# Turning the second matmul of a fused attention and feed-forward kernel round: W1 stationary, 512 tokens moving, and the output turned back by VectorE, copies and GpSimd

## Chip, cores, metric

One core of one Trainium2 chip. The metric is the device time of one execution in microseconds (us), lower is better. A run is called slow when it is over 1.5% above the fastest of the same kernel; such runs do occur on some chips at a lower granted clock, and verdicts use the fast runs alone. A verdict of "faster" or "slower" needs 2%.

## The reference, cut to what matters

```python
x: (4, 12480, 128)   inducing: (32, 128)   w_in: (128, 2048)   w_out: (2048, 128)   alpha: (2048,)

def mab(q, kv):                       # one attention head, softmax over kv
    a = softmax(q @ kv.T / sqrt(128));  return a @ kv
h   = mab(inducing, x)                # 32 rows per batch
y   = mab(x, h).reshape(49920, 128)
hid = y @ w_in
out = (maximum(hid, 0) + alpha * minimum(hid, 0)) @ w_out
```

The kernel uses that y = (softmax weights over 32) @ h. It forms hW = h @ w_in once per batch, so that a hidden unit is a sum over 32 scores only, and splits the activation into alpha * hid (a linear term, folded into one 32 x 128 matrix hA) and (1 - alpha) * max(hid, 0), whose scale is folded into W1. The softmax denominator is applied to the output at the end.

## The kernel before

Tokens are worked in groups of 512, four groups to a block of 2048, six blocks and a remainder of 192 tokens to a batch, four batches. A group takes four fills. A fill makes four PSUM banks of hidden units (each a 32-row matmul of 512 tokens; four run at once in the four row strips of the array), which ScalarE or VectorE evict with a ReLU into `gt`, and then multiplies the `gt` of the fill before with W1.

```python
def fill(st, g, j):                                # first matmul: hidden units x 512 tokens
    for r in range(4):
        ps = bank()
        mm(ps[:, :512], st.hW[32*r : 32*r+32, j, :], rep[32*r : 32*r+32, :512])
    # ... four evictions ps -> gt[:, r, :], split between ScalarE and VectorE by a plan

def mm2(st, g, j, gt):                             # second matmul: 16 of 128 columns
    for r in range(4):
        for k in range(NB):                        # NB = 4 blocks of 128 tokens
            mm(acc[:, k, :], gt[:, r, k*128 : k*128+128], W1[:, r*NJ + j, :], ...)

def finish(st, g):                                 # tokens are on partitions: scale and store
    nc.vector.tensor_tensor(out=ob, in0=acc, in1=rbc, op=MULT)        # 1 / denominator
    (nc.sync if last_one else nc.gpsimd).dma_start(out=dst, in_=ob)   # 256 KB a group

def a_load(st, u):                                 # x of the next batch, a block of 2048 tokens
    nc.gpsimd.dma_start(out=xn, in_=src)
def a_xpose(st, u):                                # the same, transposed: xT
    nc.sync.dma_start_transpose(out=st.xT[:, u], in_=xn)
def b_rep(st, s):                                  # scores, replicated to four row strips
    for r in range(4): nc.sync.dma_start(out=rep[32*r : 32*r+32], in_=e2d)

# when (in groups, k = 2 i of the batch before):  a_load at k, a_xpose at k + 3,
#   a_scores (TensorE reads xT) at k + 5, its transposed scores e1T through SyncE, a_accum at k + 8;
#   b_scores(s) and its store e2d at group 4 s - 4, b_rep at 4 s - 3, first use at group 4 s
```

Every engine's order is fixed by the program (`pin`), also that of the DMAs in the queues of SyncE and GpSimd.

The softmax here doesn't subtract the row's maximum and nothing guards it: scores larger than these inputs give would overflow.

Of the kernel before, what the change touches and what calls it, by code (L numbers as in the profile page):

```python
# [15 lines left out]
P = 128  # L16
NB = 4
GRP = P * NB
NQ = 4
# [5 lines left out]
def kernel(  # L25
# [30 lines left out]
    def pin(bi):  # L56
# [18 lines left out]
    gt_pool = ctx.enter_context(tc.tile_pool(name="gtp", bufs=4))  # L75
    head_pool = ctx.enter_context(tc.tile_pool(name="headp", bufs=3))
    rep_pool = ctx.enter_context(tc.tile_pool(name="repp", bufs=3))
    dram = ctx.enter_context(
        tc.tile_pool(name="e2d", bufs=3, space=bass.MemoryType.DRAM)
    )  # L80
    ob_pool = ctx.enter_context(tc.tile_pool(name="obp", bufs=3))
    psum = ctx.enter_context(
        tc.tile_pool(name="ps", bufs=1, space=bass.MemoryType.PSUM)
    )
# [16 lines left out]
    def new_batch(b):  # L101
        st = Batch()
        st.b = b
        st.xT = xt_pool.tile([C, NS, NQ, GRP], bf16, name="xT", tag="xT")
        st.xTr = xt_pool.tile([C, JR, PR], bf16, name="xTr", tag="xTr")
        st.xn = {}
        st.e1T = {}
        st.sc = scale
        st.rs = None
        st.e2 = {}  # L110
        st.d = {}
        st.rep = {}
        st.rden = {}
        if b > 0:
            st.es = work.tile([P, NS + 1], f32, name="es", tag="es")
            st.hacc = work.tile([P, C], f32, name="hacc", tag="hacc")
            nc.vector.memset(st.es[:], 0.0)
            nc.vector.memset(st.hacc[:], 0.0)
        return st
# [266 lines left out]
    def b_den(st, s):  # L386
        e2 = st.e2.pop(s)
        ps = bank()
        if s < NS:
            for j in range(NB):  # L390
                mm(ps[:, j * NQ : (j + 1) * NQ], e2[:, j * P : (j + 1) * P], pick[:])
            rd = work.tile([P, NB, NQ], f32, name="rd", tag="rd")
            pin(nc.vector.reciprocal(
                out=rd[:].rearrange("p j q -> p (j q)"), in_=ps[:, : NB * NQ]
            ))
        else:
            for j in range(JR):
                mm(ps[:PR, j : j + 1], e2[:, j * PR : (j + 1) * PR], pick[0:M, 0:1])
            rd = work.tile([PR, JR, 1], f32, name="rdr", tag="rdr")
            pin(nc.vector.reciprocal(  # L400
                out=rd[:].rearrange("p j q -> p (j q)"), in_=ps[:PR, :JR]
            ))
        st.rden[s] = rd
# [3 lines left out]
    def shape_of(g):  # L407
        return (P, NB, 1) if g < NS * NQ else (PR, JR, 2)

    held = []  # L410

    def flush():
        while held:
# [31 lines left out]

    def mm2(st, g, j, gt):
        pp, nb, cp = shape_of(g)
        acc = accs[(st.b * NG + g) % 2]
        begun = (g % 2 == 1 and st.b + g > 1) or cp > 1
        for r in range(4):  # L450
            for i in range(cp):
                c = r * NJ + j * cp + i
                for k in range(nb):
                    k0 = (i * nb + k) * pp
                    mm(
                        acc[:pp, k, :], gt[:, r, k0 : k0 + pp], W1[:, c, :],
                        start=(j == 0 and r == 0 and i == 0 and k == 0 and not begun),
                        stop=False, skip_group_check=True,
                    )
        if j == NJ // cp - 1 and st.b * NG + g > 0:  # L460
            held.append((st, g))
# [7 lines left out]
        return []  # L469

    def linear(st, groups):
        for k in range(NB):
            for r, g in enumerate(groups):
                pp, nb, cp = shape_of(g)
                if k < nb:
                    mm(
                        accs[(st.b * NG + g) % 2][:pp, k, :],
                        st.rep[g][32 * r : 32 * r + 32, k * pp : (k + 1) * pp],
                        st.hA[32 * r : 32 * r + 32, :],
                        start=((r == 1 or cp > 1) and k == 0), stop=False, skip_group_check=True,  # L480
                    )

    def finish(st, g):
        pp, nb, _ = shape_of(g)
        acc = accs[(st.b * NG + g) % 2]
        s, q = divmod(g, NQ)
        rd = st.rden[s]
        rq = rd[:, :, q : q + 1]
        rbc = bass.AP(tensor=rq.tensor, offset=rq.offset, ap=[rq.ap[0], rq.ap[1], [0, C]])
        ob = ob_pool.tile([P, NB, C], f32, name="ob", tag="ob")  # L490
        pin(nc.vector.tensor_tensor(  # L491
            out=ob[:pp, :nb, :], in0=acc[:pp, :nb, :], in1=rbc, op=MULT
        ))
        t0 = st.b * N + s * SUP
        if s < NS:
            dst = out[t0 : t0 + SUP, :].rearrange("(p q j) c -> q p j c", q=NQ, j=nb)[q]
        else:
            dst = out[t0 : t0 + REM, :].rearrange("(p j) c -> p j c", j=nb)
        last_one = (st.b, g) == (B - 1, NG - 1)
        pin((nc.sync if last_one else nc.gpsimd).dma_start(out=dst, in_=ob[:pp, :nb, :]))  # L500
        st.rep.pop(g)



    order = [0, 1, NS] + list(range(2, NS))
    st = new_batch(0)
    ind_f = const.tile([M, C], f32, name="ind_f")
    xs = const.tile([P, NQ, GRP], f32, name="xs")
    src = x[0, 0:SUP, :].rearrange("(p q j) c -> p q (j c)", q=NQ, j=NB)
    pin(nc.sync.dma_start(out=xs[:, 0:2, :], in_=src[:, 0:2, :]))  # L510
    pin(nc.scalar.dma_start(out=xs[:, 2:4, :], in_=src[:, 2:4, :]))
# [11 lines left out]
    for u in order[3:]:  # L523
        a_load(st, u, pieces=2)
    w_in_b = const.tile([C, DFF], bf16, name="w_in_b")
    w_out_f = const.tile([P, KC, C], f32, name="w_out_f")
    pin(nc.gpsimd.dma_start(out=w_in_b[:], in_=moe_w_in))
    w_out_v = moe_w_out.rearrange("(r j p) c -> p r j c", p=P, j=NJ)
    w_out_g = w_out_f[:].rearrange("p (r j) c -> p r j c", j=NJ)
# [150 lines left out]
    def make_plan():  # L680
# [3 lines left out]
        for i, (b, g, j) in enumerate(fills):  # L684
            pp, nb, cp = shape_of(g)
            w = pp * nb * cp
            ca, cd = w * 0.75 + 96, w * 1.04 + 68
            lin = 240 if j == NJ // cp - 1 and lin_groups(b, g) else 0
            costs = [c for _, c in tasks.get((b * NG + g, j), []) if c]
            idx = [(at_bank + r) % RING for r in range(4)]  # L690
            nxt = []
            for P_, A_, D_, free, done, hist in beam:
# [4 lines left out]
                for bits in range(1, 15):  # L697
                    for pos in (0, 2, 4) if ended else (4,):
# [19 lines left out]
                            f[k % RING] = t + 100  # L718
                            k += 1
                        if done is not None:  # L720
                            n0, c0, d0 = done
                            for r in range(4):
                                p = max(p, d0[r]) + c0 * n0 * 57
                            p += 85
                        late = sum(max(0, x - p) for x in f)
                        rank = p + 0.1 * (a + d - 2 * p) + 0.1 * late
                        nxt.append((rank, p, a, d, tuple(f), (nb, cp, dn), (hist, bits, pos)))
            nxt.sort(key=lambda x: x[0])
            beam, seen = [], set()
            for x in nxt:  # L730
                key = tuple(
                    int(max(y - x[1], -50) / 50)
                    for y in (x[2], x[3], *x[4], *x[5][2])
                )
                if key not in seen:
                    seen.add(key)
                    beam.append(x[1:])
                    if len(beam) == 60:
                        break
# [12 lines left out]
    for b, g, j in fills:  # L752
        gt = fill(states[b], g, j)
        for fn, _ in tasks.pop((b * NG + g, j), []):
            fn()
        if prev is not None:
            mm2(*prev)
        prev = (states[b], g, j, gt)
    mm2(*prev)
    flush()  # L760
    assert not tasks, tasks

# [29 lines left out]
```

## Time and profile before

| | before |
|---|---|
| time, median of 3 first runs | 594.55 us |
| span and granted clock of the profiled run | 591.6 us, 0.997 |
| TensorE busy | 98% |
| DMA moved | 70.1 MB |

Spans are a little shorter than times, since they run from the first to the last instruction. The prediction below shows the page's lines on busy engines, the chain and a round; three more views matter for what came. TensorE's waits (what it waited for, us in total, times, longest):

```profile
PE ring L549 <- DVE ind_b L546: 6.3, 1, 6.3
PE ring L171 <- DVE xn L596: 0.9, 1, 0.9
```

All of it is start-up; afterwards TensorE waits for nothing. SyncE's issues around one of the transposing loads of x (start, us to issue):

```profile
78.62 0.34 SPq L363 DMA_DIRECT2D e2d<-e  x1
80.37 1.17 SPq L274 DMA_TRANSPOSE e1Tr<-e1r  x1
81.63 2.53 SPq L142 DMA_TRANSPOSE xT<-xn  x1
84.26 3.79 SPq L371 DMA_DIRECT2D rep<-e2d  x4
```

and TensorE's first use of that load:

```profile
90.46 0.40 PE L95 MATMUL ring<-xT,IT 128*32 128x512 bf16 x4
```

The record of the load says that it landed 6.09 us after its start, at 87.72: 2.74 us to spare. I had not worked this out before predicting. Done for all 18 such loads, it gives 8 to 11 us to spare for the first of each batch, and 0.2 to 3.5 us, median 1.5, for the other fifteen. None is late, so no wait shows.

### The profile page before, as it was taken

Reading aid. Unit: us, or ns where it says so; the run is one execution under the profiler, and the core shown is the slowest. Engines: PE = TensorE matmul, PEld = TensorE weight load, DVE = VectorE, ACT = ScalarE, POOL = GpSimd, SP = SyncE. Lnnn points to the kernel's source line nnn. Section 1 sums busy time; section 2 is a strip of 40 time slices with the busy share of each in tenths; the row PEclk is TensorE's granted clock in tenths of the full one; section 3 lists DMA queues with packets and bytes.
Section 4 is the critical chain, followed back from the end, with each engine's and each line's share of the span. In section 5 each row is a group of like instructions: output and inputs, shape, how many; then the busy total and the mean of one; then the engine's idle time right before and its main releaser. Section 6 shows DMA issues by size and latency. Waiting matters only on the chain.

```text
span 591.6 us, 21747 instructions
## 1 busy us (share of the span) xinstructions
PE 578.9 (98%) x9210; PEld 434.9 (74%) x9210; DVE 517.7 (87%) x869; ACT 502.1 (85%) x987; POOL 86.5 (15%) x173
## 2 busy tenths in 40 slices
PE   5999999999999999999999999999999999999997
PEld 4677777777777777777777777777777777777776
DVE  3688998999889989998989899988988998998996
ACT  2579888888889988888889998888888988989986
POOL 6631111101011111110111111101101101101101
PEclk9899999999999999999999999999999999999999
DMA  9793969781248569953126597975122221321211
GB/s 197 186 193 90 180 145 167 152 141 55 76 96 165 125 132 180 174 135 91 60 83 139 124 162 133 181 161 133 56 73 77 94 87 60 94 84 63 92 42 62
DMA packets 81633, 70.10 MB, mean 118 GB/s; under 512 B 55440, under 2 KB 71072, under 8 KB 81536
## 3 DMA queue, kind: packets, MB, share of 16 engines
q0 software_dynamic: 12768, 39.30, 26.7%
q1 hardware_dynamic: 68624, 28.89, 25.8%
q8 instruction: 72, 1.18, 0.8%
q10 hardware_dynamic: 144, 0.52, 0.3%
q14 instruction: 25, 0.20, 0.1%
HBM read 40.20 MB, written 28.75 MB: 117 GB/s over the span
## 4 chain that ended last, share of the span: by engine, by line
PE 96%; ACT 1%; DMA 1%; DVE 1%; issue 0%; SPq 0%; ACTq 0%
PE acc L95 68%; PE ring L95 27%; PE ring L171 1%; DMA ind_f<-in_inducing_dram 1%; ACT gt L440 1%; DVE xT L177 0%; DVE ob L491 0%; DVE gt L442 0%; ACT rep L381 0%; DVE xn L596 0%; ACT xT L179 0%; ACT e L353 0%; SPq L510 0%; ACT e1t L196 0%; DVE ind_b L546 0%
## 5 line engine op out<-in xcount | busy, mean ns | idle before, releaser
L440 ACT ACTIVATE gt<-ring 128x512 bf16<-128x512 f32 x899 | 469.5, 599 | 69.1 <-PE ring L95 28.1
L442 DVE TENSOR_SCALAR gt<-ring 128x512 bf16<-128x512 f32 x669 | 434.9, 685 | 53.6 <-PE ring L95 39.1
L95 PE MATMUL acc<-W,gt 128*128 128x128 bf16 x6272 | 419.1, 220 | 0.2 <-DVE ob L491 0.2
L95 PEld LDWEIGHTS <-gt 128*128 128x128 bf16 x6272 | 353.4, 98 | 79.7 <-issue 77.0
L95 PE MATMUL ring<-rep,hW 32*128 32x512 bf16 (+1 forms) x1600 | 157.5, 380 | 0.5 <-DVE hW L247 0.2
L500 POOL DMA_DIRECT2D out_dram<-ob x99 | 53.4, 540 | 490.1 <-DVE ob L491 426.2
L95 PEld LDWEIGHTS <-hW 32*128 32x128 bf16 x1600 | 41.1, 91 | 42.3 <-DVE hW L247 1.2
L491 DVE TENSOR_TENSOR ob<-acc,rd 128x512 f32<-128x512 f32 x96 | 65.4, 681 | 2.5 <-PE acc L95 2.5
L95 PE MATMUL acc<-hA,rep 32*128 32x128 bf16 x392 | 19.8, 214 | 0.0
L95 PEld LDWEIGHTS <-rep 32*128 32x128 bf16 x392 | 15.6, 94 | 5.6
L128 POOL DMA_DIRECT2D xn<-in_x_dram x28 | 15.3, 551 | 3.6 <-DMA xn<-in_x_dram 2.7
L196 ACT ACTIVATE e1t<-ring 128x256 bf16<-128x256 f32 (+1 forms) x13 | 4.8, 371 | 10.0 <-PE ring L95 9.9
L177 DVE COPY xT<-ring 128x1024 bf16<-128x1024 bf16 (+1 forms) x12 | 8.0, 669 | 4.6 <-PE ring L171 4.1
L353 ACT ACTIVATE e<-ring 128x512 bf16<-128x512 f32 x18 | 11.0, 612 | 0.0
L261 ACT ACTIVATE e<-ring 128x512 bf16<-128x512 f32 x18 | 10.9, 605 | 0.0
L95 PE MATMUL ring<-xT,hT 128*32 128x512 bf16 (+1 forms) x98 | 10.5, 391 | 0.0
L171 PE MATMUL ring<-ident,xn 128*128 128x128 bf16 x96 | 8.8, 249 | 0.9 <-DVE xn L596 0.9
L171 PEld LDWEIGHTS <-xn 128*128 128x128 bf16 x96 | 6.8, 112 | 1.0 <-DVE xn L596 1.0
L95 PE MATMUL ring<-xn,e1T 128*32 128x128 bf16 x288 | 7.4, 221 | 0.0
L95 PEld LDWEIGHTS <-hT 128*32 128x32 bf16 (+1 forms) x122 | 3.7, 93 | 4.9 <-issue 2.4
L95 PE MATMUL ring<-xT,IT 128*32 128x512 bf16 x72 | 7.2, 390 | 0.0
L95 PEld LDWEIGHTS <-e 128*128 128x128 bf16 x96 | 4.0, 97 | 3.2 <-issue 1.1
(84 smaller groups left out, 106.4 us busy)
## 6 DMA issues: line engine op xcount, KB each, us to landing
out_dram<-ob POOLq DMA_DIRECT2D x96, 256.0 KB, 2.8
rep<-e2d SPq DMA_DIRECT2D x92, 128.0 KB, 3.4
xn<-in_x_dram POOLq DMA_DIRECT2D x18, 512.0 KB, 6.4
e2d<-e SPq DMA_DIRECT2D x24, 128.0 KB, 2.2
xn<-in_x_dram POOLq DMA_DIRECT2D x10, 256.0 KB, 8.6
w_out_f<-in_moe_w_out_dram POOLq DMA_DIRECT2D x4, 256.0 KB, 11.0
xs<-in_x_dram ACTq DMA_DIRECT2D x1, 512.0 KB, 4.9
xs<-in_x_dram SPq DMA_DIRECT2D x1, 512.0 KB, 5.1
```

Source lines behind the costliest of these rows:

```text
L95: return pin(nc.tensor.matmul(o, lhsT, rhs, start=start, stop=stop, **kw))
L128: pin(nc.gpsimd.dma_start(out=xn[:, i * w : (i + 1) * w, :], in_=src[:, i * w : (i + 1) * w, :]))
L171: pin(nc.tensor.transpose(tp[:, k * P : (k + 1) * P], xn[:, q, j * C : (j + 1) * C], ident[:]))
L177: pin(nc.vector.tensor_copy(out=dst, in_=tp[:, :w]))
L196: pin(nc.scalar.activation(out=e1t[:pp, :nb, :].rearrange("p k m -> p (k m)"), in_=ps[:pp, : nb * M], func=EXP, scale=scale,))
L261: pin(nc.scalar.activation(out=e1[:], in_=ps[:], func=EXP, scale=scale, accum_out=st.es[:, u : u + 1]))
L353: pin(nc.scalar.activation(out=e2[:], in_=ps[:], func=EXP, scale=scale_of(st)))
L440: pin(nc.scalar.activation(out=gt[:, r, :w], in_=ps[:, :w], func=RELU))
L442: pin(nc.vector.tensor_relu(gt[:, r, :w], ps[:, :w]))
L491: pin(nc.vector.tensor_tensor(out=ob[:pp, :nb, :], in0=acc[:pp, :nb, :], in1=rbc, op=MULT))
L500: pin((nc.sync if last_one else nc.gpsimd).dma_start(out=dst, in_=ob[:pp, :nb, :]))
```

## The change

Intent: sixteen 128-column matmuls with gt stationary become four 512-column ones with W1 stationary. That spares TensorE twelve instructions' overhead a fill. The result then has channels on partitions and must be turned back: VectorE transposes 32x32 blocks out of PSUM in place of its scaling, sixteen SBUF-to-SBUF copies per block of 2048 tokens (64 KB each, two after each fill, from SyncE's queue) put the blocks where they belong, GpSimd scales by the denominators and stores 1 MB per block. 92 of the 100 groups are turned; the remainders and the last block are not.

```diff
 def mm2(st, g, j, gt):
     for r in range(4):
+        if turned(st.b, g):
+            mm(flat(acc), W1[:, r * NJ + j, :], gt[:, r, :], ...)
+            continue
 def finish(st, g):
+    if turned(st.b, g):
+        turn(st, s, q, acc)
+        return
+def turn(st, s, q, acc):
+    pin(nc.vector.transpose(out=yT[:, :, q]..., in_=acc[:]...))
+    if q < NQ - 1:
+        return
+    def shuffle(a, k):
+        pin(nc.sync.dma_start(
+            out=yq[32 * a : 32 * a + 32, k], in_=yT[32 * k : 32 * k + 32, a]))
+    def leave():
+        for q in range(NQ):
+            pin(nc.gpsimd.tensor_tensor(out=ob[:, q]..., in0=yq[:, :, q]..., in1=..., op=MULT))
+        pin(nc.gpsimd.dma_start(out=out[t0 : t0 + SUP, :]..., in_=ob[:]...))
+    for a in range(4):
+        for k in range(4):
+            moves.append(lambda a=a, k=k: shuffle(a, k))
+    moves.append(leave)
 for b, g, j in fills:
     gt = fill(states[b], g, j)
     for fn, _ in tasks.pop((b * NG + g, j), []):
         fn()
+    move(2)
     if prev is not None:
         mm2(*prev)
```

Cut: the linear term (two 512-column matmuls in place of eight), buffers (three for rd; two instead of three for the 256 KB outputs `ob`; xs and w_out_f share yT's room), and the constants of the plan that splits the evictions.

More of the change, by code (lines that the diff above doesn't have):

```diff
@@ L77 @@
     rep_pool = ctx.enter_context(tc.tile_pool(name="repp", bufs=3))
+    rd_pool = ctx.enter_context(tc.tile_pool(name="rdp", bufs=3))
     dram = ctx.enter_context(
@@ L80 @@
     )
-    ob_pool = ctx.enter_context(tc.tile_pool(name="obp", bufs=3))
+    ob_pool = ctx.enter_context(tc.tile_pool(name="obp", bufs=2))
+    wide_pool = ctx.enter_context(tc.tile_pool(name="widep", bufs=2))
     psum = ctx.enter_context(
@@ L113, in new_batch @@
         st.rden = {}
+        st.yT = {}
         if b > 0:
@@ L391, in b_den @@
                 mm(ps[:, j * NQ : (j + 1) * NQ], e2[:, j * P : (j + 1) * P], pick[:])
-            rd = work.tile([P, NB, NQ], f32, name="rd", tag="rd")
+            rd = rd_pool.tile([P, NB, NQ], f32, name="rd", tag="rd")
             pin(nc.vector.reciprocal(
@@ L408, in shape_of, with turned, acc_of, flat @@
         return (P, NB, 1) if g < NS * NQ else (PR, JR, 2)
+    def turned(b, g):
+        return g < NS * NQ and (b, g // NQ) != (B - 1, NS - 1)
+    def acc_of(b, g):
+        return accs[(b * NG + g) % 2]
+    def flat(acc):
+        return acc[:].rearrange("p k c -> p (k c)")
     held = []
+    moves = []
+    def move(n):
+        for _ in range(min(n, len(moves))):
+            moves.pop(0)()
     def flush():
@@ L447, in mm2 @@
         pp, nb, cp = shape_of(g)
-        acc = accs[(st.b * NG + g) % 2]
+        acc = acc_of(st.b, g)
         begun = (g % 2 == 1 and st.b + g > 1) or cp > 1
         for r in range(4):
+            if turned(st.b, g):
+                mm(
+                    flat(acc), W1[:, r * NJ + j, :], gt[:, r, :],
+                    start=(j == 0 and r == 0 and not begun),
+                    stop=False, skip_group_check=True,
+                )
+                continue
             for i in range(cp):
@@ L471, in linear @@
     def linear(st, groups):
+        for r, g in enumerate(groups):
+            if turned(st.b, g):
+                mm(
+                    flat(acc_of(st.b, g)), st.hA[32 * r : 32 * r + 32, :],
+                    st.rep[g][32 * r : 32 * r + 32, :],
+                    start=(r == 1), stop=False, skip_group_check=True,
+                )
         for k in range(NB):
@@ L474, in linear @@
                 pp, nb, cp = shape_of(g)
-                if k < nb:
+                if k < nb and not turned(st.b, g):
                     mm(
@@ L484, in finish @@
         pp, nb, _ = shape_of(g)
-        acc = accs[(st.b * NG + g) % 2]
+        acc = acc_of(st.b, g)
         s, q = divmod(g, NQ)
+        st.rep.pop(g)
+        if turned(st.b, g):
+            turn(st, s, q, acc)
+            return
         rd = st.rden[s]
@@ L500, in finish @@
         pin((nc.sync if last_one else nc.gpsimd).dma_start(out=dst, in_=ob[:pp, :nb, :]))
-        st.rep.pop(g)
+    def turn(st, s, q, acc):
+        if q == 0:
+            st.yT[s] = wide_pool.tile([P, 4, NQ, NB, 32], f32, name="yT", tag="yT")
+        yT = st.yT[s]
+        pin(nc.vector.transpose(
+            out=yT[:, :, q, :, :].rearrange("p a j c -> p j a c"),
+            in_=acc[:].rearrange("p j (a c) -> p j a c", a=4),
+        ))
+        if q < NQ - 1:
+            return
+        yq = wide_pool.tile([P, 4, NQ, NB, 32], f32, name="yq", tag="yq")
+        def shuffle(a, k):
+            pin(nc.sync.dma_start(
+                out=yq[32 * a : 32 * a + 32, k], in_=yT[32 * k : 32 * k + 32, a]
+            ))
+        def leave():
+            rd = st.rden[s]
+            ob = wide_pool.tile([P, NQ, NB, C], f32, name="obw", tag="obw")
+            for q in range(NQ):
+                rq = rd[:, :, q : q + 1]
+                pin(nc.gpsimd.tensor_tensor(
+                    out=ob[:, q].rearrange("p j (k c) -> p j k c", k=4),
+                    in0=yq[:, :, q].rearrange("p k j c -> p j k c"),
+                    in1=bass.AP(
+                        tensor=rq.tensor, offset=rq.offset,
+                        ap=[rq.ap[0], rq.ap[1], [0, 4], [0, 32]],
+                    ),
+                    op=MULT,
+                ))
+            t0 = st.b * N + s * SUP
+            pin(nc.gpsimd.dma_start(
+                out=out[t0 : t0 + SUP, :].rearrange("(p q) c -> p (q c)", p=P),
+                in_=ob[:].rearrange("p q j c -> p (q j c)"),
+            ))
+        for a in range(4):
+            for k in range(4):
+                moves.append(lambda a=a, k=k: shuffle(a, k))
+        moves.append(leave)
     order = [0, 1, NS] + list(range(2, NS))
@@ L507 @@
     ind_f = const.tile([M, C], f32, name="ind_f")
-    xs = const.tile([P, NQ, GRP], f32, name="xs")
+    xs = wide_pool.tile([P, NQ, GRP], f32, name="xs", tag="yT")
     src = x[0, 0:SUP, :].rearrange("(p q j) c -> p q (j c)", q=NQ, j=NB)
@@ L525 @@
     w_in_b = const.tile([C, DFF], bf16, name="w_in_b")
-    w_out_f = const.tile([P, KC, C], f32, name="w_out_f")
+    w_out_f = wide_pool.tile([P, KC, C], f32, name="w_out_f", tag="yT")
     pin(nc.gpsimd.dma_start(out=w_in_b[:], in_=moe_w_in))
@@ L687, in make_plan @@
             ca, cd = w * 0.75 + 96, w * 1.04 + 68
-            lin = 240 if j == NJ // cp - 1 and lin_groups(b, g) else 0
+            m2 = 216 if turned(b, g) else nb * cp * 57
+            lin = 216 if j == NJ // cp - 1 and lin_groups(b, g) else 0
             costs = [c for _, c in tasks.get((b * NG + g, j), []) if c]
@@ L720, in make_plan @@
                         if done is not None:
-                            n0, c0, d0 = done
+                            c0, d0 = done
                             for r in range(4):
-                                p = max(p, d0[r]) + c0 * n0 * 57
+                                p = max(p, d0[r]) + c0
                             p += 85
@@ L726, in make_plan @@
                         rank = p + 0.1 * (a + d - 2 * p) + 0.1 * late
-                        nxt.append((rank, p, a, d, tuple(f), (nb, cp, dn), (hist, bits, pos)))
+                        nxt.append((rank, p, a, d, tuple(f), (m2, dn), (hist, bits, pos)))
             nxt.sort(key=lambda x: x[0])
@@ L732, in make_plan @@
                     int(max(y - x[1], -50) / 50)
-                    for y in (x[2], x[3], *x[4], *x[5][2])
+                    for y in (x[2], x[3], *x[4], *x[5][1])
                 )
@@ L759 @@
     mm2(*prev)
+    move(len(moves))
     flush()
```

## The prediction

> **What bounds the kernel now.** I read the page first: busy shares, the slices, then the chain that ended last.
>
> ```profile
> PE 578.9 (98%) x9210; PEld 434.9 (74%) x9210; DVE 517.7 (87%) x869; ACT 502.1 (85%) x987; POOL 86.5 (15%) x173
> PE 96%; ACT 1%; DMA 1%; DVE 1%; issue 0%; SPq 0%; ACTq 0%
> PE acc L95 68%; PE ring L95 27%; PE ring L171 1%; DMA ind_f<-in_inducing_dram 1%; ACT gt L440 1%; DVE xT L177 0%; DVE ob L491 0%; DVE gt L442 0%; ACT rep L381 0%; DVE xn L596 0%; ACT xT L179 0%; ACT e L353 0%; SPq L510 0%; ACT e1t L196 0%; DVE ind_b L546 0%
> ```
>
> TensorE is 96% of the chain, and 68% is the second matmul (into acc), the part that the change rewrites. A busy TensorE alone proves little, so I then read the list of waits for TensorE: after the start it waits on nothing worth a microsecond, so the time is its own issue rate. The timeline gives that rate:
>
> ```profile
> 212.44 0.40 PE L95 MATMUL ring<-rep,hW 32*128 32x512 bf16 x4
> 212.77 1.07 PE L95 MATMUL acc<-W,gt 128*128 128x128 bf16 x16
> 213.77 0.40 PE L95 MATMUL ring<-rep,hW 32*128 32x512 bf16 x4
> 214.09 1.07 PE L95 MATMUL acc<-W,gt 128*128 128x128 bf16 x16
> ```
>
> One round (I call it a fill) is four concurrent 32-row matmuls of 512 columns, then sixteen 128-column ones: 212.44 to 213.77 is 1.33 us. Single records, start to start: 10 ns for the four together, 317 from the last of them to the first acc matmul, 15 steps of 56.6 on average (median 56) = 849, and 151 from the last acc matmul to the next round. Sum 1.327 us, the median round. The 317 and the 151 each contain one streaming time (213 and 53 ns) plus about 100 ns for the change between the two array layouts.
>
> The engines behind TensorE are not far away. A group (four fills) on VectorE:
>
> ```profile
> 199.59 0.68 DVE L491 TENSOR_TENSOR ob<-acc,rd 128x512 f32<-128x512 f32 x1
> 200.31 4.73 DVE L442 TENSOR_SCALAR gt<-ring 128x512 bf16<-128x512 f32 x7
> 204.96 0.68 DVE L491 TENSOR_TENSOR ob<-acc,rd 128x512 f32<-128x512 f32 x1
> ```
>
> Seven evictions and one scaling: 7 x 0.608 (start to start, back to back) + 0.718 = 4.98 us of the group's 5.31. ScalarE does nine evictions at 0.477 = 4.3 us.
>
> **What the Trainium skill says.** (1) "TensorE: Matmul & The Clock Gate", section "Wait — 56ns, not 53.3ns?": back to back, a warm matmul starts every N/2.4 GHz plus about 2.5 ns, 55.6 ns at N=128 and 215.7 at N=512. The trace agrees at 128 (56); it has no full-height 512-column stream, so 215.7 is taken from the page. (2) "VectorE: DVE Perf Modes", "The three transpose paths": the VectorE transpose works in 32x32 blocks only and takes 311 ns for 128x128 bf16. Nothing in this trace shows one. At 0.96 GHz that is 298 cycles, 128 elements and 170 fixed, so my estimate for 512 fp32 elements is 682/0.96 = 710 ns if fp32 goes at one element a cycle; the scaling it replaces took 681. (3) "SBUF — State Buffer", "Who interferes with whom": a VectorE instruction with at most one SBUF input, outside the two-port modes, does not contend with GpSimd. VectorE's evictions and transposes read PSUM, so the scaling on GpSimd should not slow them; no run shows it yet. (4) "DMA: Bandwidth & Descriptors", "Issuing engines are not separate DMA queues": all queues run on the same 16 engines, so the new copies share them with the input loads. The trace has both kinds side by side (26.7% and 25.8% of the engines).
>
> **The change part by part.**
>
> Second matmul: 92 of 100 groups are turned (all but the four remainders and the last block of four), 4 fills each = 368 fills. Each loses sixteen 128-column matmuls and gets four 512-column ones with W1 stationary, the same columns in all. New: three steps of 216 = 648, then the last one's streaming, 213, plus the same ~100 ns change of layout, about 314; 962 instead of 849 + 151 = 1000. Saving 38 to 39 ns a fill; the weight loads (1472 for 5888) hide under a 213 ns stream. 368 x 0.039 = 14.4 us, all on the path, so **580.2 us** if nothing else moves. So little because the columns stay: only 12 x 2.5 to 3.3 ns of step overhead goes. The linear term (two 512-column matmuls for eight of 128 per pair of groups) stays near 0.31 us.
>
> VectorE: 92 transposes for 92 scalings, 710 for 681 ns by the estimate, and the split of evictions stays at 661 of VectorE and 875 of ScalarE in the built program. A group on VectorE becomes about 5.0 us of 5.15 without other tasks. It still fits, with 0.15 us to spare.
>
> GpSimd: 92 multiplications of 128x512. The row for W1's scaling (same size, broadcast factor) is 1047 ns, so 96 us of 580, and 69 fewer output DMAs to issue. Off the path.
>
> DMA: 23 blocks x 16 = 368 copies of 64 KB inside SBUF in 2 KB pieces, 24 MB more beside 70 MB. From queue 0's row (39.3 MB in 26.7% of 16 engines), 24.1 MB is about 16% more load, 53% to some 70% on average. But in some slices the engines already show 90% and above, and two 5 us windows (345 to 355 us) show 0.98 and 1.25.
>
> SyncE's queue is where I expect a loss. It issues in order, at 0.43 us a plain DMA, and in the built program each waits until the DMA eight places before it has landed (eight semaphores, used in turn). In the first three batches the order before a block's replicated scores (rep) becomes: store of e2, 2 copies, transposed load, 2 copies, the big transposing load of x, 4 copies, then the four rep loads. The list of SyncE's DMAs before shows what that meets: the x load takes 2.4 to 4.4 us to issue and lands 5.6 to 8.5 us after its start. With 6 copies between (2.6 us), and the fourth rep load bound to the x load's landing (it is eighth behind), I estimate rep lands 3 to 4 us later than now, more where the engines are full. Rep's last landing to its first use now is 4.1 to 5.4 us for most of these nine blocks, but 2.5 and 3.5 us for blocks 2 and 3 of the third batch (for instance landing at 352.49, use at 354.99). So I expect waits of 0 to 2 us in some four to six of the nine blocks, **about 3.3 us in all**. Sum: 594.55 - 14.4 + 3.3 = 583.5 us.
>
> **The rivals.**
>
> A: rep is never late; the whole 14 us arrives, about 580. For it: the slack is above 4 us in seven of nine blocks, and the fourth batch has none of these x loads. Against it: the 2.5 us of one block.
>
> B: the transpose is slow on fp32 (half rate, about 1.2 us). Then a VectorE group is about 5.5 us, above TensorE's 5.15; VectorE sets the end, some 0.35 us x 92 = 32 us more: about 605 to 612. For it: no trace shows an fp32 transpose. Against it: the page's one-number figure fits a cycle per element.
>
> C: the DMA engines, not the queue's order, are the bound in batches 0 to 2: copies, loads and rep all slow each other, rep takes 7 us or more as it did once (7.42 us at 365.66), and waits of 2 to 3 us appear in all nine blocks: 590 to 598. For it: the full slices. Against it: these blocks move 1 MB of copies in some 22 us, little beside what 16 engines do.
>
> D: the evictors, with 0.15 us to spare in a group on VectorE, make TensorE wait a little in each group: up to 0.1 us x 92 = 9 us, about 589.
>
> **Range and chances.** Faster by over 2% means below 582.7, a mere 2.5 us above the best case. A with small waits (about 0.4) falls there; the expected case, C and D fall within 2% (0.5); B and a bad C can be slower than 606.4 (0.1). Predicted 583.5 us, eight in ten between 577 and 596.
>
> **What will show it.** Acc matmuls of 512 columns start 216 ns apart, x1472, and a quiet round is 1.285 to 1.29 us: the first step is right. If a round is still 1.32, the layout change grew. StreamTranspose at 680 to 760 ns: B is out; 1.1 us or more, B it is, with VectorE at 95% and TensorE waiting on VectorE. TensorE waits on rep's landing at the start of blocks 2 to 4 of batches 0 to 2 and none in the last batch: the queue's step is right; with copies landing in 2 to 3 us it is the order of the queue, with 5 us or more it is C. Waits of TensorE on ScalarE or VectorE evictions spread over all groups: D. I am wrong outright if the time is below 577 (the layout change shrinks too) or above 596.

## The result, and the profile after

Before 594.57 us (594.38 to 597.48), after **603.84 us** (601.26 to 604.26). Ratio 1.0135, 95% interval 1.0093 to 1.0178: slower by 1.35%, "same" by the 2% rule, but outside the predicted range. (A ratio here is the mean time of one kernel's fast runs over that of the other's of the same rounds, so not quite the ratio of the medians quoted.) The profiled spans are 591.6 and 601.8 us, the mean granted clocks 0.997 and 0.984. The answer of the profile after to the lines that the prediction quoted, from the page (busy engines; the chain by engine and by line):

```profile
PE 574.0 (95%) x4518; PEld 209.8 (35%) x4518; DVE 517.7 (86%) x869; ACT 502.2 (83%) x987; POOL 143.7 (24%) x196
PE 80%; DMA 11%; SPq 3%; ACT 2%; issue 2%; POOL 1%; DVE 0%; POOLq 0%; DVEq 0%; ACTq 0%
PE acc L97 56%; PE ring L97 23%; DMA xT<-xn 7%; DMA xn<-in_x_dram 3%; SPq L550 2%; ACT gt L457 2%; DMA winT<-w_in_b 1%; DMA out_dram<-ob 1%; SPq L374 1%; POOL obw L559 1%; DMA e2d<-e 0%; SPq L657 0%; SPq L268 0%; POOL xn L131 0%; DVE yT L541 0%
```

TensorE, 96% of the chain before, is 80%; a DMA that was on no chain, xT<-xn, has 7%. The rounds, in the timeline of TensorE:

```profile
216.38 0.40 PE L97 MATMUL ring<-rep,hW 32*128 32x512 bf16 x4
216.71 1.04 PE L97 MATMUL acc<-gt,W 128*128 128x512 bf16 x4
217.68 0.40 PE L97 MATMUL ring<-rep,hW 32*128 32x512 bf16 x4
```

216.38 to 217.68 is 1.30 us, where it was 1.33: the change does what it is for. The turning back, in the page's groups (busy us, mean ns of one | idle before) and its DMA issues (KB each, us to landing):

```profile
L559 POOL TENSOR_TENSOR obw<-yq,rd 128x512 f32<-128x512 f32 x92 | 93.3, 1038 | 407.3 <-DMA yq<-yT 274.8
L541 DVE STREAM_TRANSPOSE yT<-acc 128x512 f32<-128x512 f32 x92 | 65.0, 706 | 1.9 <-PE acc L97 1.9
yq<-yT SPq DMA_DIRECT2D x368, 64.0 KB, 2.2
```

All near what was expected. TensorE's waits are not:

```profile
PE ring L97 <- DMA xT<-xn: 9.2, 6, 3.6
PE ring L625 <- DVE ind_b L622: 6.2, 1, 6.2
```

Six waits for the transposed x. No line for rep. Three of the six are long: before 92.81, 236.25 and 380.70 us, each time the third load of a batch. The timeline of TensorE over the first of them:

```profile
90.08 0.40 PE L97 MATMUL ring<-rep,hW 32*128 32x512 bf16 x4
92.81 0.40 PE L97 MATMUL ring<-xT,IT 128*32 128x512 bf16 x4 [2.33 <-DMA xT<-xn]
...
94.26 0.61 PE L97 MATMUL ring<-rep,hW 32*128 32x512 bf16 x4
...
96.63 0.61 PE L97 MATMUL ring<-rep,hW 32*128 32x512 bf16 x4
```

After the wait of 2.33 us a round, 94.26 to 96.63, takes 2.37 us. The stretch view shows why (start:end, length, busy us of PE, PEld, DVE, ACT, POOL, then granted clock, DMA share, GB/s):

```profile
94.00:97.00 3.00, 3.00 (x13) 0.65 (x12) 1.31 (x2) 1.57 (x3) 0.00 (x0) 0.50 0.68 199
```

The clock is halved from 93.91 to 97.32 us, 3.41 us, and likewise with the two other long waits (237.27 to 240.68, 380.63 to 384.04). So such a wait costs its own length and then some 1.55 us more: 3.41 us at 1.30/2.37 of the pace. (A stretch of this kind also falls in the start-up of both kernels, at 26.05 us before and 25.64 after; it is no part of the loss.)

The issues of SyncE and of GpSimd before that wait:

```profile
75.92 2.42 SPq L550 DMA_DIRECT2D yq<-yT  x4
78.82 1.06 SPq L366 DMA_DIRECT2D e2d<-e  x1
79.92 1.90 SPq L550 DMA_DIRECT2D yq<-yT  x2
81.92 1.41 SPq L277 DMA_TRANSPOSE e1Tr<-e1r  x1
83.38 1.21 SPq L550 DMA_DIRECT2D yq<-yT  x2
84.69 5.85 SPq L145 DMA_TRANSPOSE xT<-xn  x1
90.59 2.49 SPq L550 DMA_DIRECT2D yq<-yT  x4
93.18 1.98 SPq L374 DMA_DIRECT2D rep<-e2d  x4
```

```profile
77.01 0.60 POOL L569 DMA_DIRECT2D out_dram<-obw  x1 [0.30 <-POOL obw L559]
77.60 1.07 POOL L131 DMA_DIRECT2D xn<-in_x_dram  x2
```

The load of x starts at 84.69 instead of 81.63, though TensorE came to want it at the same time (90.48, before 90.46), and lands after 8.08 us instead of 6.09. So it is 3.04 us later in the queue, counted from the want, and 1.99 longer under way, 5.03 together; less the 2.74 it had to spare, that is 2.29 of the 2.33 that TensorE waited. The three long waits taken apart so (this splits them, and is no test of a cause):

| third load of a batch | issue later, against the want | longer to landing | to spare before | sum | waited |
|---|---|---|---|---|---|
| first, wait to 92.81 | 3.04 us | 1.99 | 2.74 | 2.29 | 2.33 |
| second, to 236.25 | 2.50 | 1.79 | 2.18 | 2.11 | 2.16 |
| third, to 380.70 | 2.52 | 1.29 | 0.29 | 3.52 | 3.56 |

The other fifteen loads of x land sooner than before, after 4.35 us in the median instead of 7.08, so it is not the engines' mean load that delays these three.

Why longer under way: GpSimd sent a store of 1 MB and two loads in one burst at 77.01 to 78.67. From the single packets' records (packets started and KB moved in each 2 us; a table made from them, not a view):

```
             GpSimd's queue      SyncE's queue
after  80-82     58, 475 KB         12,   8 KB
       82-84     91, 307            16,  33
       84-86    102, 352            90,  92
       86-88     84, 336            88,  86
       88-90     27,  53           272, 261
       90-92      0,   0          1877, 481
before 82-84      2,   4           911, 232
       84-86     23,  94          1093, 280
```

From 84 to 88 us the two queues get packet for packet, and GpSimd's are larger; alone, SyncE's gets twenty times as many. The load of x itself is not what flies beside the burst. Its packets are the ones of 256 bytes, some 2,000 of them, and nearly all start between 90.0 and 92.5 us, when GpSimd's queue is empty. Until then SyncE's queue was still sending what had been issued before the load: the e2 store of 78.82 landed at 89.30, the copies of 79.92 and 81.16 at 90.51 and 90.82. So in these 8.08 us the load mostly stood behind a backlog of its own queue, which the burst had held up.

The end of the program changed too. The chain of what ended last, after, and its last working piece before:

```profile
588.01 0.10 POOL obw L559
...
592.36 0.58 POOL out_dram L569
...
593.10 4.50 DMA out_dram<-ob
```

```profile
587.98 0.42 DVE ob L491
```

The last matmul ends at 593.09 us and the span at 601.8, 8.7 us later; before, at 587.95 and 591.6, 3.7 later. The last turned block's scaling on GpSimd begins at 588.01, its 1 MB store at 592.36, and the last outputs stand behind it.

**Budget.** Rounds: 30 ns each (median 1.326 to 1.296) times 368, or 34 ns as the blocks of the last batch give it: minus 11 to 12 us. Start, where four loads now go out together (that this is the cause was not tested): plus 1.3. Waits for xT: plus 9.2. Three stretches at half clock: plus 4.7. That is 3 to 4 us; the last matmul ends 5.1 later, so 1 to 2 us are unassigned. Tail: plus 5.0. Sum measured: 10.2 in the spans.

### The profile page after: what moved, and what is told of

It reads as the page before. It is cut to its first block, busy times and chain, and to the rows that moved or that the text cites. A ratio compares the mean times of both kernels' runs of the same rounds, so it can differ in the third digit from the quotient of the medians.

```text
span 601.8 us, 12844 instructions
## 1 busy us (share of the span) xinstructions
PE 574.0 (95%) x4518; PEld 209.8 (35%) x4518; DVE 517.7 (86%) x869; ACT 502.2 (83%) x987; POOL 143.7 (24%) x196
## 3 DMA queue, kind: packets, MB, share of 16 engines
q1 hardware_dynamic: 86288, 53.03, 38.7%
q0 software_dynamic: 8720, 39.29, 24.3%
## 4 chain that ended last, share of the span: by engine, by line
PE 80%; DMA 11%; SPq 3%; ACT 2%; issue 2%; POOL 1%; DVE 0%; POOLq 0%; DVEq 0%; ACTq 0%
PE acc L97 56%; PE ring L97 23%; DMA xT<-xn 7%; DMA xn<-in_x_dram 3%; SPq L550 2%; ACT gt L457 2%; DMA winT<-w_in_b 1%; DMA out_dram<-ob 1%; SPq L374 1%; POOL obw L559 1%; DMA e2d<-e 0%; SPq L657 0%; SPq L268 0%; POOL xn L131 0%; DVE yT L541 0%
## 5 line engine op out<-in xcount | busy, mean ns | idle before, releaser
L97 PE MATMUL acc<-gt,W 128*128 128x512 bf16 x1472 | 385.2, 385 | 0.3 <-DVE yT L541 0.3
L559 POOL TENSOR_TENSOR obw<-yq,rd 128x512 f32<-128x512 f32 x92 | 93.3, 1038 | 407.3 <-DMA yq<-yT 274.8
L97 PEld LDWEIGHTS <-W 128*128 128x128 bf16 x1472 | 115.2, 98 | 165.6 <-issue 77.2
L97 PE MATMUL ring<-rep,hW 32*128 32x512 bf16 (+1 forms) x1600 | 160.0, 382 | 0.5 <-DVE hW L250 0.2
L541 DVE STREAM_TRANSPOSE yT<-acc 128x512 f32<-128x512 f32 x92 | 65.0, 706 | 1.9 <-PE acc L97 1.9
L97 PE MATMUL acc<-W,gt 128*128 128x128 bf16 (+1 forms) x384 | 25.6, 220 | 0.0
L97 PEld LDWEIGHTS <-gt 128*128 128x128 bf16 (+1 forms) x384 | 21.9, 106 | 4.2 <-issue 3.8
L97 PE MATMUL acc<-rep,hA 32*128 32x512 bf16 x92 | 17.6, 374 | 0.0
L569 POOL DMA_DIRECT2D out_dram<-obw x23 | 13.7, 596 | 6.8 <-POOL obw L559 6.8
L535 POOL DMA_DIRECT2D out_dram<-ob x7 | 3.8, 537 | 25.9 <-DVE ob L526 25.8
```

The costliest lines, as they stand in the source:

```text
L97: return pin(nc.tensor.matmul(o, lhsT, rhs, start=start, stop=stop, **kw))
L541: pin(nc.vector.transpose(out=yT[:, :, q, :, :].rearrange("p a j c -> p j a c"), in_=acc[:].rearrange("p j (a c) -> p j a c", a=4),))
L559: pin(nc.gpsimd.tensor_tensor(out=ob[:, q].rearrange("p j (k c) -> p j k c", k=4), in0=yq[:, :, q].rearrange("p k j c -> p j k c"), in1=ba ...
L569: pin(nc.gpsimd.dma_start(out=out[t0 : t0 + SUP, :].rearrange("(p q) c -> p (q c)", p=P), in_=ob[:].rearrange("p q j c -> p (q j c)"),))
```

## The experiments

Theory 1, at first: the burst of loads in GpSimd's queue delays xT. Theory 2: the tail is the order of GpSimd's last stores. Theory 3: the place of the copies in SyncE's queue makes xT late. (The recorded expectations of e1_pace, e3_pace_tail and e4_onecopy still call this one "Theory 2", and that of e2_tail counts the tail under "Theory 1".) Rival to all three: 24 MB more are too much for the DMA engines wherever they are issued. Four kernels ran in each of the first two calls, three in the third, one in the last. In the second call the chip was noisy: only two of seven runs of the kernel before were fast (594.31, 602.33), so its kernels are best compared with the changed kernel in the same rounds, e7_again.

### e1_pace: spread the loads

```diff
-                at(k, lambda n=n, u=u: a_load(states[n], u))
+                at(k, lambda n=n, u=u: (pace(), a_load(states[n], u)))
+    def pace():        # one column of the current fill's gt: GpSimd can't run ahead
+        pin(nc.gpsimd.tensor_copy(out=tick[:], in_=now[0][:, 3, 0:1]))
```

> Edit: each input load on GpSimd's queue first waits, through a one-column GpSimd copy, for the current round's evicted tile, so loads go out one by one again, two groups apart, and not in pairs behind the 1 MB output. Theory 1 (bunching: the in-order GpSimd queue, no longer paced by the output DMAs, sends 1 MB of output and two loads in one burst that fills the DMA engines for some 10 us, and the transposing load of x lands late): the waits of TensorE on xT fall from about 9 us to under 1.5 us, the half-clock stretches of 3.4 us inside the run disappear, time 603.8 - 13 = about 590 us, with the tail of 5 us still there. Theory 2 (the 368 copies in SyncE's queue delay it by their number and bytes): nothing changes much, 601 to 604 us.

Correct, 607.97 us, ratio 1.0211 [1.0133, 1.0289]. TensorE's waits:

```profile
PE ring L97 <- DMA xT<-xn: 7.6, 3, 4.4
PE ring L97 <- DMA rep<-e2d: 2.6, 8, 0.4
```

Theory 1 failed in this form: spreading the loads brought nothing. But this is no clean test of the burst. The loads went out at 63.33, 78.27 and 87.34 us, the first just ahead of rep loads, the second 0.7 us after the 1 MB store at 77.55, so that a smaller burst remained; the load of x, issued at 83.55, landed 10.5 us later, worse than before the edit. No run shows what the copies cost with no burst at all.

### e2_tail: the last stores from SyncE

```diff
-        last_one = (st.b, g) == (B - 1, NG - 1)
+        last_one = st.b == B - 1 and g >= NG - 5
```

> Edit: the four untouched groups of the last block send their output from SyncE's queue, not from GpSimd's, where the last scaling stands in front of them. Theory 1: the last 10 us lose the 5.8 us wait of VectorE for an output buffer: time falls by 4 to 5 us to about 599 us, the xT waits stay. If the tail is due to the order of the work itself (TensorE ends late anyway) it falls by less than 1 us.

Correct, 603.69 us, ratio 1.0115 [1.0027, 1.0203]. Its profile fell in the slow state (610.07), so only its tail is read: 7.4 us, 1.3 less than 8.7, where 4 to 5 were expected. The order of the last stores is a small part.

### e3_pace_tail: both

> Edit: both edits of the two runs before. Theory 1: both gains add, about 585 to 586 us, that is 1.5% under the kernel before: what the turned matmul saves (368 rounds x 30 ns = 11 us) less about 1 us at the start. Theory 2: about 599 us, the tail alone.

Correct, 608.33 us, ratio 1.0221 [1.0128, 1.0313]. As with the two alone: the pacing gains nothing, the tail stays (6.9 us). Here the last turned block's copies landed at about 590.5, its scaling ran from 590.95 to 595.0 and its store was issued at 595.31: the tail hangs on copies, scaling, store, in this order.

### e4_onecopy: one copy instead of sixteen (wrong result on purpose)

```diff
-        for a in range(4):
-            for k in range(4):
-                moves.append(lambda a=a, k=k: shuffle(a, k))
+        for _ in range(15):
+            moves.append(lambda: None)
+        moves.append(lambda: shuffle(3, 3))      # the scaling waits for it, and reads yT
```

> Edit, wrong result on purpose: of the 16 copies inside SBUF only the last is made, at its old place, and the scaling reads the unshuffled tile but still waits for that copy, so GpSimd's queue keeps its times and its burst of one output and two loads while SyncE's queue loses 15 of 16 copies. Theory 2 (copies): the xT waits go, about 589 to 591 us. Theory 1 (burst): the burst stays and the xT transposes still land 8 us or more after their issue, but they are issued some 3 us earlier, so part of the waits remain: 593 to 600 us.

587.48 us, ratio 0.9863 [0.9754, 0.9971], fast runs 583.57 to 588.92 (a fourth run was slow, 604.68), profiled span 581.7 at clock 0.999.

```profile
PE ring L97 <- DMA xT<-xn: 0.3, 1, 0.3
```

No half clock in mid-run, though GpSimd's burst (store at 69.78, two loads up to 70.91) is still there. So the copies are needed for the loss, and the burst alone doesn't make it. Without them a gain of the size of the matmul part arrives: the mean of the three fast runs is 9.4 us under that of the kernel before in the same rounds (586.18, 595.57). It isn't the matmul part alone, since this run's profile also lacks the half clock in the start-up, some 1.5 us. It doesn't tell the copies' number in the queue from their bytes.

### e5_poolq: the same copies from GpSimd's queue

```diff
         def shuffle(a, k):
-            pin(nc.sync.dma_start(
+            pin(nc.gpsimd.dma_start(
```

> Edit: the 368 copies inside SBUF are issued from GpSimd's queue; SyncE's queue is in order and length again what it was before the change, and the bytes stay the same. Theory 3 (the copies' place ahead of the transposing load in SyncE's in-order queue, which is served one packet for each packet of GpSimd's queue while that sends a burst): the xT waits go, about 585 to 588 us. Rival (16 DMA engines have too much to do, whatever queue asks): waits stay, 598 us or more. It also puts the copies behind the input loads in GpSimd's queue, so the loads may come later: if that is what matters, waits on xT reappear.

Correct. Fast runs 586.54 and 587.93, two others slow (597.3, 598.57); ratio 0.9815 with an interval too wide to use, [0.9528, 1.0102]. Against e7_again of the same rounds (mean 603.34) the fast runs are 0.973. TensorE's wait for xT:

```profile
PE ring L97 <- DMA xT<-xn: 0.9, 3, 0.4
```

The same 24 MB now go through GpSimd's queue (42.6% of the engines' time, 24.3% in the changed kernel; SyncE's 25.0%, 38.7%), and the long waits and the half clock are gone. That speaks for theory 3 and against the rival that the engines are too full, as far as this run goes; e11_poolq limits it.

### e6_small: sixteen copies of a sixteenth of the bytes (wrong on purpose)

```diff
-                out=yq[32 * a : 32 * a + 32, k], in_=yT[32 * k : 32 * k + 32, a]
+                out=yq[32 * a : 32 * a + 32, k, 0, 0, :], in_=yT[32 * k : 32 * k + 32, a, 0, 0, :],
```

> Edit, wrong result on purpose: the 16 copies stay in their places on SyncE's queue, but each moves 128 B a partition in place of 2 KB (the same number of DMAs and packets, one sixteenth of the bytes); the scaling reads the unshuffled tile and waits for the small copies. If number and place in the queue cost the time (theory 3): 598 us or more, xT waits as in the changed kernel. If the 24 MB cost it: about 586 us.

590.64 us, ratio 0.9881 [0.9755, 1.0007]; 0.980 of e7_again. (Cut above: the scaling reads yT, after four small copies that wait for the moved pieces.)

```profile
PE ring L97 <- DMA xT<-xn: 3.3, 5, 1.1
```

Between the two: as many places in the queue with hardly any bytes leave five waits, none over 1.1 us, and none halves the clock. So the place in the queue makes xT late, the bytes make it later, and no wait of this length comes with the half clock.

### e7_again: the changed kernel, unedited

> The changed kernel again, unedited, beside the three others on the same chip: 1.013 to 1.016 times the kernel before, as on record.

603.06 us, ratio 1.0084 [0.9959, 1.0209]; xT waits of 10.0 us in five, half clock with each of the three long ones. The time and the waits repeat. The ratio, against two fast runs of the kernel before that lie 8 us apart, is not clear of 1.

### e8_xfirst: the load of x one group earlier

```diff
-                at(k + 3, lambda n=n, u=u: a_xpose(states[n], u))
+                at(k + 2, lambda n=n, u=u: a_xpose(states[n], u))
```

> Edit: the transposing load of x is put one group (four rounds, some 5 us) earlier in the program, so it stands ahead of the block's copies in SyncE's queue where it stood behind 12 of them. Theory 3: the long xT waits (2.5 to 3.9 us once a batch) and the half-clock stretches go, time falls by 8 to 13 us to 590 to 595 us on the changed kernel's own scale. Rival (engines too full): the waits shift to rep or stay, less than 4 us gained.

Correct, 596.13 us, ratio 0.9955 [0.9792, 1.0117]; 0.988 of e7_again, so 7.5 us gained. SyncE's issues and TensorE's wait:

```profile
73.17 1.71 SPq L145 DMA_TRANSPOSE xT<-xn  x1
...
84.18 6.70 SPq L550 DMA_DIRECT2D yq<-yT  x6
90.98 1.97 SPq L374 DMA_DIRECT2D rep<-e2d  x4
```

```profile
PE ring L97 <- DMA rep<-e2d: 2.6, 8, 0.6
```

All waits for xT are gone, no half clock in mid-run, and now TensorE waits for rep: eight times, at most 0.6, 2.6 us in all, in five of the nine blocks. This is near what the prediction had put in its sum for rep (3.3, four to six blocks), though in another order of the queue, so it is no proof of that sum. In the changed kernel itself rep is on time, but barely: from the last landing to its first use the nine blocks have 0.05 to 2.4 us to spare, where they had 2.5 to 5.4. In three of the nine this is due to the long wait for xT just ahead (2.2 to 3.6 us, and the slow clock after it): without it, by my estimate from these numbers, rep would have been some 2 to 3 us late there.

### e11_poolq: e5_poolq once more, five rounds, another chip

> The same kernel as e5_poolq (the 368 copies issued from GpSimd's queue, SyncE's order as before the change), measured again because the chip of that run was in its slow state for half of the time. Theory (the copies' place in SyncE's queue makes the transposing load of x late, and each long wait also halves the clock): fast runs at 586 to 588 us, ratio to the kernel before about 0.987, no TensorE wait on xT over 1 us, no half clock in mid-run. Rival (the two fast runs of e5_poolq were luck; the 24 MB cost it wherever they are issued): 595 us or more.

598.62 us, five fast runs 592.50 to 599.57, ratio 1.0037 [0.9991, 1.0083]. A miss: not 586 to 588, and by the time alone the rival (595 us or more) did better; by the trace the picture is mixed.

```profile
PE ring L97 <- DMA xT<-xn: 4.6, 4, 2.9
```

One long wait is back (TensorE stands until 244.99, then half clock from 245.22 to 248.63). The load of x, issued at 233.73 with a 1 MB store at 234.18 and an input load at 234.77, took 11.2 us to land. By the single packets, 714 and 846 of SyncE's queue started in the two us before the store's first packets came at 237, and 9 to 56 in each us from 238 to 244. So with the copies in GpSimd's queue the place in SyncE's queue is given back, but here a store and a load of that queue meet xT in flight, and its margin is so thin that the same program loses or keeps it. e5_poolq's two fast runs were the good side of this.

### e10_fasttail: faster copies in the last batch

```diff
-        move(2)
+        move(4 if b == B - 1 else 2)
```

and the edit of e2_tail.

> The changed kernel, with the copies of the last batch issued four a fill instead of two and the four untouched groups of the last block stored from SyncE. In the last batch SyncE has no transposing loads of x to delay. Theory of the tail (last turned block's copies, then its scaling on GpSimd, then its 1 MB store set the end): the scaling is done some 5 us earlier, the tail after the last matmul shrinks from 8.7 to 4 or 5 us, time about 599 to 600. The three long waits for xT with half clock stay as they are. Rival (the tail is the time in which one 1 MB store and the stores of ob share the engines, or a fixed closing time of the program): tail 7 us or more, time 603.

Correct, 598.85 us, ratio 1.0074 [1.0041, 1.0108]. Its waits for xT are the old ones (9.4 us in six), the last matmul ends at 594.33 and the span at 599.8: a tail of 5.5 us instead of 8.7. GpSimd's last piece:

```profile
590.54 0.59 POOL L569 DMA_DIRECT2D out_dram<-obw  x1 [0.30 <-POOL obw L559]
```

The store is now issued before the last matmul ends. The theory of the tail holds for 3.2 us of its 5.0.

### e9_best: copies from GpSimd's queue, faster tail

> Both: copies on GpSimd's queue, four a fill in the last batch, the last block's stores from SyncE. If the two losses are separate and add up: 586.5 to 588 less 1 to 3 us, 583 to 586 us, ratio 0.981 to 0.985, tail of 3.5 to 5 us, no half clock in mid-run. If the tail is not set by the copies' lateness: 587, as e11_poolq.

Correct, **586.86 us**, fast runs 585.06 to 588.07, ratio to the kernel before **0.986 [0.983, 0.989]**, on the chip and in the rounds of e11_poolq.

```profile
PE ring L97 <- DMA xT<-xn: 1.3, 3, 0.6
```

The tail is 3.5 us. It is 1.4% under the kernel before, clear of noise, though "same" by the 2% rule; the changed kernel did not run in these rounds (e10_fasttail, its nearest kin there, is at 1.0074). But up to the last batch its program is that of e11_poolq, whose five fast runs are 4 us or more slower; the tail explains 2.5. Why its waits for xT stayed short in this run and e11_poolq's did not, the edit doesn't explain, and I leave it open.

### e12_all: e9_best with the load of x one group earlier

> e9_best with the big transposing load of x asked for one group (about 5.2 us) earlier, as in e8_xfirst. In e9_best TensorE still waited 1.3 us on xT, and in e11_poolq once 3.2 us with half clock after it, so the margin of that load is thin even with the copies on GpSimd's queue. Theory: the xT waits go to zero; the replicated scores, which had 0.6 to 3 us to spare in e9_best, keep most of that because SyncE no longer issues the copies; no half clock in mid-run; 582 to 586 us, ratio 0.980 to 0.985, fast runs closer together than those of e11_poolq. Rival (the load only changes places with the scores' stores and copies, which become late instead, as in e8_xfirst): waits on rep of 1 to 3 us, time as e9_best or slower, 586 to 589.

Correct, on yet another chip with three slow runs of six (up to 632.16); fast runs 588.46 to 594.63, ratio 0.9926 [0.9855, 0.9996]. The expectation failed. The chain of the profiled run (594.63):

```profile
225.41 20.81 DMA xT<-xn
```

A load of x, usually 4 to 9 us to landing, took 20.8; the load before it took 12.0, and three later ones 14.3 to 18.0, so this was no single event. Packets of SyncE's queue took 0.15 to 0.20 us each from 230 to 236 us, three to four times as long as before (0.05), and little was moved (50 GB/s). TensorE waited 5.6 us. Whether the earlier load met the copies in a bad way or something from outside disturbed this chip, one profile can't tell: open.

## Why the prediction was wrong

**What bounds the kernel** held: TensorE's own issue rate.

**The saving per round** was mis-sized: 39 ns predicted, 30 measured by the median round. By single records the four-matmul run starts with a step of 226 ns, then 216 and 216, and 311 to the next round: 969, where 962 was reckoned. The old run begins with a step of 66 ns and goes on in steps of 56; the average of 56.6 had swallowed that 10 ns, and I gave the new run none. With the 10 + 317 at the head unchanged, that is 1.296. 3 us of 14.4 gone.

**VectorE and GpSimd** were right: 706 ns for 710, 1038 for 1047, the evictions' split unchanged, no wait of TensorE on an evictor worth naming. Rivals B and D are out.

**SyncE's queue** is the step that failed, and in one respect only: the tile. "I estimate rep lands 3 to 4 us later than now" was about right as a delay: in the nine blocks rep has 1.2 to 4.8 us less to spare than before, 3.3 on average, and the third xT load of each batch came 3.8 to 5.0 us later relative to its want. But I had worked out the slack for rep alone (2.5 to 5.4 us), and called xT merely one of the things that delay rep. xT stands ahead of rep in the same queue, behind the same copies, and had 0.3 to 2.7 us at these places. Nor had I asked what GpSimd's stores of 1 MB, sent in one burst with the loads, would hold up: 1.3 to 2.0 us of the lateness. So the waits came at xT, 9.2 us in six, and rep, for which 3.3 us were expected, had none. e8_xfirst, which takes xT out of the way, shows waits for rep of that size, 2.6 us.

(One reading there is a little off: over all 18 loads, the load of x took 1.3 to 4.4 us to issue and 5.1 to 8.5 to land. Nothing hangs on it.)

**What a wait costs** was missing. I counted waits at their length. With each of the three long ones TensorE's clock was also halved for 3.41 us, 1.55 us more. e6_small and e8_xfirst, with waits up to 1.1 us, show none of this in mid-run. Over all traces, every wait of TensorE of 1.93 us or more after the first 30 us went with such a stretch, and no single wait of 0.8 to 1.61 us did. Yet length alone is not the rule: in e1_pace the clock was halved from 220.52 to 223.93 us after two waits for rep of 0.38 and 0.35 us, with TensorE busy for 2.66 of the 3.5 us before.

**The tail** was missing altogether: 5.0 us. The prediction looked at what lies beside TensorE's work in the middle of the run, not at what remains when TensorE is done: copies two a fill, then 4 us of scaling, then 1 MB. e10_fasttail takes back 3.2 of it.

**Rival C** ("the DMA engines, not the queue's order") is partly true and not as it was put. e5_poolq and e4_onecopy show that the loss isn't the mean load; e6_small shows that the copies' bytes lengthen xT's way, e11_poolq that a store and a load of the other queue do. Waits came at xT, not in all nine blocks at rep. The prediction had also named its own failure ("wrong outright ... above 596"), and so it was.

Put together: 594.6 - 11 or 12 + 1.3 + 9.2 + 4.7 + 5.0 = 603 to 604, and 1 to 2 us stay unassigned.

The pages cited: the step of 216 ns at 512 columns is confirmed by the trace ("TensorE: Matmul & The Clock Gate", "Wait — 56ns, not 53.3ns?" states 215.7). "DMA: Bandwidth & Descriptors", section "Queues, rings and completion order", says that an engine takes the queues in turn, a packet from each; 178 packets of SyncE's queue beside 186 of GpSimd's between 84 and 88 us agree. From 80 to 84 us, with copies issued and not landed, it was 28 beside 149, which this does not explain. This page would have told me to look at what else is sent while a queue holds many small packets. The two other statements that the prediction took: VectorE's evictions kept their mean of 684 ns (685 before) beside GpSimd's 93.3 us of scaling, as "SBUF — State Buffer" has it; and the transpose estimate of 710 ns was met by 706, from a single figure of the page and the guess of one element a cycle.

## What to carry to other kernels

Before putting more DMAs into an in-order queue, list everything that stands behind them with its slack (landing to first use), also the tiles that are never waited for; the one with the least slack decides, not the one you think of. Count a wait of TensorE of about 2 us or more dearer than its length, and follow a new path of the output to the very end of the program. A gain of 2% on the engine that bounds is easily lost to transfers that were on time by 1.5 us.

## What the Trainium skill lacked or had wrong

- "TensorE: Matmul & The Clock Gate", section "Back-to-back issue gap": it gives a sustained 131 ns per matmul at N=512 with weight loads between, and calls the 216 ns formula an over-count there. Here a stream of four with a new weight each runs at steps of 226, 216 and 216 ns (368 such streams); 131 is not seen.
- Same page: the first step of a run after matmuls of another array layout is 10 ns longer (66 for 56, 226 for 216), and the change of layout costs about 100 ns beyond the streaming each way (317 into, 311 or 151 out of the run). Neither is there. "TensorEngine Tiling (Array Packing)", section "Key Properties", does say that a change of tiling mode drains TensorE, but gives no time.
- Same page, "What's actually happening" and its advice for kernels (no idle gaps over about 3 us): the clock halved with waits of 1.93 us (e9_best, at 36.33), 2.07 (e10_fasttail), 2.16 and 2.33 us already, for 3.41 us at least, and in e1_pace after two of 0.38 and 0.35 us; one of 1.61 us (e3_pace_tail) did nothing. The length of the slow stretch agrees with the page's window.
- "VectorE: DVE Perf Modes", "The three transpose paths": no figure for fp32 or for a PSUM source. ("Vector Engine (DVE) Microarchitecture Reference", section 3.8, has the rate, one element a cycle and lane, but no time of an instruction.) 128x512 fp32 out of PSUM took 706 ns (x92), hardly more than the scaling that it replaced (681).
- "DMA: Bandwidth & Descriptors", "Issuing engines are not separate DMA queues": it says that another issuing engine saves only the time on the sequencer, usually small. Here the same 368 copies moved from SyncE to GpSimd took the fast runs (two only) from 603 to 587 us on one chip, by e8_xfirst because of what stood behind them in order; on another chip most of it didn't come (592.5 to 599.6).
